# Denominators' absolute value and 128x1 products on another engine, with a new order of issue, in an xLSTM and mixture-of-experts kernel

## The chip, the cores and the metric

The kernel runs on one core of one Trainium2 chip. The metric is device time in microseconds (us) of one execution; a profiled execution is also known by its span, the time from the first to the last instruction of the program.

The engines are TensorE (PE in the profile, with PEld for its weight loads), VectorE (DVE), ScalarE (ACT), GpSimd (POOL) and SyncE (SP, which only issues transfers here).

## The reference

Three layers follow each other. The first is a recurrent attention over 768 positions of 2 batches and 8 heads of width 40, the second a feed-forward layer with a rational activation, the third a dense mixture of 4 experts with a ReLU.

```python
def _attn_ref(q, k, v, i_gate, f_gate, o_gate):
    for t in range(S):
        m_new = np.maximum(f_gate[:, :, t] + m, i_gate[:, :, t])
        f_stab = np.exp(f_gate[:, :, t] + m - m_new)
        i_stab = np.exp(i_gate[:, :, t] - m_new)
        C = f_stab * C + i_stab * outer(vt, kt)
        n = f_stab * n + i_stab * kt
        h_tilde = C @ qt
        denom = np.maximum(np.abs(n @ qt), 1.0)
        y[:, :, t] = sigmoid(o_gate[:, :, t]) * h_tilde / denom

def _moe_ref(x, w_in, w_out, a, b):          # x: 1536 x 320, w_in: 320 x 2048
    h = x @ w_in
    P = a[0] + a[1] * h + a[2] * h**2 + a[3] * h**3
    Q = 1.0 + np.abs(b[0]) * np.abs(h) + np.abs(b[1]) * h**2
    return (P / (Q + 1e-06)) @ w_out

def _moe2_ref(x, domain_probs, w1, w2):      # 4 experts, 320 x 1024 and 1024 x 320
    p = domain_probs / (domain_probs.sum(-1, keepdims=True) + 1e-09)
    for e in range(4):
        out += p[:, e:e + 1] * (np.maximum(x @ w1[e], 0.0) @ w2[e])
    return out
```

## The kernel before

The attention is done in chunks of 128 positions: 12 steps, 6 chunks of 2 batches. A step broadcasts the decays of the gates over the partitions (tiles `bc`, `bf`, `cb` in PSUM), turns them into a triangular weight with a scan (`fb`, line 710), multiplies the scores `sc` with it (L742), and sums the state's and the chunk's contributions in `o` (L756 and L762). Column 40 of each head of `o` is the product with the state's norm, and from it `s_pv` makes the 8 denominators of a row: `den` is max(-o, 1) by L764, then the larger of that and max(o, 1) by L765. `s_y` takes the reciprocal (L790), multiplies it into the output gate, and this into `o`. `s_x` transposes the result into `x`, as a high and a low half (L807 to L810), because every matrix product is made from two halves so that it keeps more bits.

Beside these steps the weights of the second layer are loaded and converted (`conv64`, tiles `cv_p`, `cv_l`, `cv_t`, `win`, `wout`). The second layer then runs in blocks of 256 tokens: first products `h` (L829), the rational activation `e_mono` (L853 to L868), second products `acc` (L841). It needs `x`, and `sb1`, the square root of |b[1]|, which `small_consts` makes on 128x1 tiles: an approximate square root and one step of Newton (L672 to L679). The first expert has the same form (L829, L877, L841); experts 1 to 3 use fewer products on sums of blocks (L1152), with second products at L1186. At the very end 6 accumulators `acc[t]`, each the sum of many products of L1186, are each scaled and added to `so` by VectorE (`evac_exp`, L953) and sent out by SyncE (L955).

What sets the order. Program text emits units in the order of the list `EMIT`. For each engine, `ORDER` then gives a permutation of the numbers of its own instructions, counted from 0 as they were emitted, and each instruction is tied behind the one in front of it in that list. An engine works its list strictly in order. `CHOICE` holds one letter for each use of a small operation that several engines could do (V VectorE, A ScalarE, G GpSimd), in the order of use: `ge` the masked copies of the gates, `gm` and `gl` other gate products, `ke` the products `kend` of keys and decay, `vi` the copies of the input gate, `low` and `hi` parts of the conversion, `ri` the linear part of the rational activation, `su`, `mh`, `ml` its sums and halves, `ws` the sums of weights for experts 1 to 3. `SPINS` says how many products of the identity with itself (L591, into a tile that is about to be written) are put ahead of which product.

```python
def spin(t, key):
    for _ in range(SPINS.get(key, 0)):
        PE.matmul(t[:, 0:P], spin_in, spin_in, start=True, stop=True)
...
# second(), the last 36 products of TensorE in order of emission, t = 0 to 5, six each
if k == NK - 1 and a == 1 and n == 2:
    evac_exp(e, b * NC + p * NH + w, acc[t])
```

Of the kernel before, what the change touches and what calls it, by code (L numbers as in the profile page):

```python
# [10 lines left out]
AF = mybir.ActivationFunctionType  # L11
ALU = mybir.AluOpType
# [23 lines left out]
    861-876 841-844 995 989 996 990-991 997 992 998 993 999 994 1000 880-895 1001 877-879 1002-1005 1007 1006 1008
    1013-1014 1009-1012 1019 920 896-911 949-960 1020 1015 1021 1016 1022 1017-1018 1023-1024 933-948 1025 1034 1028
    1026-1027 1040-1042 1029-1030 1035-1036 1031 1037-1038 1032-1033 1039 1049 1043-1047 1050-1053 1048 961-976 1055
    1082-1083 1054 1098-1100 1084 1079-1080 1101-1102 1081 1085-1086 1056-1059 1061-1065 1060 1066 1073-1074
    1130-1132 1067-1069 1075 1070 1076 1071 1077-1078 1072 1181-1196 1103-1113 1087-1097 1197-1212 1114-1129 1235  # L40
    1229-1232 1236-1237 1233 1238-1240 1234 1247 1241 1248-1249 1242 1250-1251 1243-1244 1213-1217 1252 1245-1246
    1218-1228 1133-1140 1733 1727 1734-1735 1728-1730 1736 1731 1737-1738 1732 1141-1142 1253-1267 1317 1268
    1143-1148 1323-1325 1318 1326 1319-1321 1327-1328 1322 1269-1284 2343 2349 2344-2345 2350-2351 2346 2352 2347
    2353-2354 2348 1329 1335 1330-1331 1336-1338 1332-1333 1339-1340 1334 1401 1285-1299 1149 1300 1402 1407 1403
    1408 1404-1405 1409-1411 1406 1412 1419 1413-1414 1420-1421 1415-1416 1422-1423 1417-1418 1424 1301-1316 2355
    2361-2363 2356 1463-1465 1457-1458 1466-1467 1459-1461 1468 1462 1341-1356 2364-2366 2357-2360 1165-1180 1150
    1425-1440 1357 1709 1703-1705 1710 1706 1389-1390 1711-1712 1707 1713-1714 1708 1151-1155 1358-1360 1156 1391
    1361 1392 1441-1456 1157-1160 1362-1365 1393-1394 1507-1508 1469-1471 1161-1164 1366-1368 1395-1400 1513
    1509-1510 1514-1515 1511 1516-1517 1512 1518 1472-1478 1519 1369 1525 1479-1487 1721 1715 1722 1716 1723-1724
    1717-1718 1488-1490 1725 1719 1726 1720 1526 1520-1521 1527-1529 1522-1523 1530 1524 1559-1571 1531 1572-1574  # L50
    1532 1537-1538 1373-1374 1539-1541 1533-1536 1542 1599-1614 1575 1581 1375-1377 1576-1579 1582-1583 1580
    1584-1586 1593-1597 1587-1591 1598 1592 1370-1372 1378-1388 1615-1630 1820 1814-1815 1821 1816 1822 1817 1823
    1818 1824 1819 1825 1669 1663-1664 1670 1665-1666 1671-1673 1667 1674 1668 1631-1634 1675 1681 1635-1645
    1676-1677 1682 1491-1498 1646 2041 1683 1678 1684-1686 2042 1679-1680 1499-1506 2047-2048 1687-1702 1543-1548
    2043 2049 2044-2046 2050-2052 1647-1650 1549-1552 1651-1652 1739-1741 1764 1758-1760 1765-1766 1653 1767
    1553-1557 1742-1757 1770 1776 1771-1772 1558 1654 1777-1778 1773 1779 1774 1780 1775 1781 1761 1768 1762-1763
    1769 1782-1797 1829 1835-1838 1830-1832 1839 1833 1840 1834 1655-1659 1798-1813 1841 1847-1848 1842 1849-1850
    1897 1660-1662 1843 1898-1903 1844 1851 1845 1852 1846 2146-2147 2140 2148 2141 2149 2142 2150 2143 2151 1853
    1826-1828 1904 2144 1905-1906 2145 1859-1860 1854-1855 1861 1907-1911 1862-1863 1856-1857 1864 1858 1865-1880
# [1256 lines left out]
```

## Time and profile before

| | |
|---|---|
| time, median of 3 runs | 631.87 us (630.75 to 633.73) |
| the profiled execution's own time | 631.61 us |
| its span | 629.8 us |
| mean granted clock of TensorE | 0.985 of full |
| TensorE busy | 609.9 us, 4417 instructions |
| VectorE busy | 479.0 us, 834 instructions |
| ScalarE busy | 367.4 us, 671 instructions |
| GpSimd busy | 274.1 us, 304 instructions |

Busy time is the time in which at least one instruction of the engine runs. Rows of a group of instructions give the busy time of the group and the mean duration of one; instructions of one engine can overlap, so that the first is less than the second times the count. Idle time stands behind, with what ended it.

### The profile page before, as it was taken

What the parts mean: (1) busy time and instruction counts of PE and PEld (TensorE: products, weight loads), DVE (VectorE), ACT (ScalarE), POOL (GpSimd) and SP (SyncE); (2) the same over time, 40 slices, a digit from 0 to 9 for tenths busy, and PEclk for the clock granted to TensorE, in tenths of its full rate; (3) what the DMA queues carried; (4) which work ended last, traced back from release to release, by engine and by line L of the source; (5) the groups of instructions that cost most, each with busy time, mean ns of one, the idle gap of its engine ahead of it and who ended that gap; (6) DMA issues with size and microseconds to landing.
All of it is one profiled execution on the core that took longest, in us unless ns stands there. A gap on an engine that the chain in (4) does not pass through costs nothing.

```text
span 629.8 us, 11629 instructions
## 1 busy us (share of the span) xinstructions
PE 609.9 (97%) x4417; PEld 596.2 (95%) x4417; DVE 479.0 (76%) x834; ACT 367.4 (58%) x671; POOL 274.1 (44%) x304
## 2 busy tenths in 40 slices
PE   7689999999999999999999999999999999999996
PEld 6678999999999999999999999989999999999996
DVE  7989999999989879787789855877555467643634
ACT  3888888747886866666678536425443253523231
POOL 5697888856643352132321237323552233531010
PEclk9679999999999999999999999999999999999999
DMA  7876344030312000000000120222120011100101
GB/s 207 275 231 170 113 120 119 21 119 2 88 42 71 1 1 2 2 1 1 1 2 22 39 81 21 55 65 69 39 69 15 14 37 46 41 2 0 63 1 62
DMA packets 21959, 36.65 MB, mean 58 GB/s; under 512 B 3568, under 2 KB 14320, under 8 KB 21904
## 3 DMA queue, kind: packets, MB, share of 16 engines
q1 hardware_dynamic: 21904, 35.92, 19.4%
q8 instruction: 34, 0.56, 0.4%
q14 instruction: 21, 0.17, 0.1%
HBM read 32.76 MB, written 1.97 MB: 55 GB/s over the span
## 4 chain that ended last, share of the span: by engine, by line
PE 86%; DVE 7%; issue 1%; DMA 1%; POOL 1%; SPq 1%; ACT 1%; DVEq 0%; ACTq 0%; POOLq 0%
PE h L829 21%; PE acc L841 20%; PE acc L1186 19%; PE h L1152 18%; PE o L762 2%; PE sc L737 2%; PE tx L807 1%; PE o L756 1%; DVE fb L710 1%; DMA stg_a<-in_moe_w_in_dram 1%; DVE gbc L331 1%; PE dl L777 1%; PE bf L649 1%; SPq L1078 1%; DVE cv_t L452 1%
## 5 line engine op out<-in xcount | busy, mean ns | idle before, releaser
L1152 PE MATMUL h<-ar,ar 128*128 128x384 f32 (+1 forms) x408 | 107.2, 341 | 0.7 <-DVE ar L1173 0.7
L829 PE MATMUL h<-x,win 128*128 128x256 f32 x768 | 104.5, 284 | 0.0
L841 PE MATMUL acc<-wout,g 128*128 128x320 f32 x576 | 101.2, 313 | 0.0
L1186 PE MATMUL acc<-ar 128*128 128x320 f32 x432 | 100.0, 309 | 0.8 <-ACT ar L1168 0.8
L829 PEld LDWEIGHTS h<-x,win 128*128 128x128 f32 x768 | 98.2, 191 | 1.0 <-DVE s__1241 L868 0.2
L1186 PE MATMUL acc<-ar,ar 128*128 128x320 f32 x432 | 98.2, 309 | 0.4 <-DVE ar L1173 0.4
L1168 ACT ACTIVATE ar<-h 128x384 fp32r<-128x384 f32 x72 | 35.3, 490 | 94.5 <-DVE h L1245 33.9
L841 PEld LDWEIGHTS acc<-wout,g 128*128 128x128 f32 x576 | 87.3, 189 | 1.1 <-POOL g L331 0.3
L1186 PEld LDWEIGHTS acc<-ar 128*128 128x128 f32 x432 | 74.7, 188 | 1.3 <-ACT ar L1168 1.3
L1186 PEld LDWEIGHTS acc<-ar,ar 128*128 128x128 f32 x432 | 74.0, 188 | 1.1 <-DVE ar L1173 0.7
L1152 PEld LDWEIGHTS h<-ar,ar 128*128 128x128 f32 (+1 forms) x408 | 71.6, 188 | 2.4 <-DVE ar L1173 1.1
L1173 DVE SCALAR_TENSOR_TENSOR ar<-h,ar 128x384 fp32r<-128x384 f32 x72 | 40.0, 556 | 35.3 <-ACT ar L1168 28.9
L1241 POOL TENSOR_TENSOR ar<-c,ar 128x384 fp32r<-128x384 f32 x24 | 24.4, 1015 | 79.5 <-ACT ar L1240 73.1
L1152 PE MATMUL h<-x,ar 128*128 128x384 f32 x216 | 57.5, 340 | 0.0
L829 PE MATMUL h<-x,we 128*128 128x256 f32 x384 | 56.3, 284 | 0.0
L829 PEld LDWEIGHTS h<-x,we 128*128 128x128 f32 x384 | 51.5, 191 | 0.1
L841 PE MATMUL acc<-we,g 128*128 128x320 f32 x288 | 49.7, 310 | 0.0
L841 PEld LDWEIGHTS acc<-we,g 128*128 128x128 f32 x288 | 43.6, 188 | 0.2 <-DVE g L878 0.2
L1152 PEld LDWEIGHTS h<-x,ar 128*128 128x128 f32 x216 | 37.3, 188 | 1.0 <-ACT s L1222 0.3
L1226 DVE TENSOR_TENSOR u<-h,s 128x384 f32<-128x384 f32 x24 | 13.3, 556 | 26.7 <-PE h L1152 22.1
L1238 ACT ACTIVATE c<-c 128x384 f32<-128x384 f32 x24 | 12.5, 522 | 36.0 <-DVE c L1237 36.0
L762 PEld LDWEIGHTS o<-v,fb 128*128 128x128 f32 x192 | 25.1, 201 | 3.9 <-DVE fb L742 3.3
(818 smaller groups left out, 1278.5 us busy)
## 6 DMA issues: line engine op xcount, KB each, us to landing
stg_b<-in_moe_w_out_dram SPq DMA_DIRECT2D x10, 512.0 KB
stg_a<-in_moe_w_in_dram SPq DMA_DIRECT2D x8, 512.0 KB
kv<-in_kv_dram SPq DMA_DIRECT2D x12, 320.0 KB
qkt<-in_qk_dram SPq DMA_DIRECT2D x24, 160.0 KB
stg_w<-in_moe_w_dram SPq DMA_DIRECT2D x12, 320.0 KB
stg_m<-in_moe_w_dram SPq DMA_DIRECT2D x24, 128.0 KB
stg_r<-in_moe_w_dram SPq DMA_DIRECT2D x72, 32.0 KB
so<-in_o_gate_dram SPq DMA_DIRECT2D x6, 320.0 KB
```

Source lines behind the costliest of these rows:

```text
L331: return ENG[alt(kind)].tensor_tensor(out=out, in0=in0, in1=in1, op=op)
L737: PE.matmul(sc[j][:, p, :], qkt[b][r, p, 2 * j], qT[r, p], start=True, stop=True)
L762: PE.matmul(o[:, h, :], st["W"][:, h, :], v1[:, h, :], start=(c == 0 and h == 0), stop=(h == H - 1))
L829: PE.matmul(o, w5[:, j, fs], r, start=(n == 0), stop=(n == len(seq) - 1))
L841: PE.matmul(acc[t], x, y, start=(first and a == 0 and n == 0), stop=(last and a == nff - 1 and n == 2))
L1152: PE.matmul(bank, w, x, start=(first and n == 0), stop=(n == 3), skip_group_check=True)
L1168: A.activation(g[:, 0], c, AF.Relu)
L1173: V.scalar_tensor_tensor(out=g[:, 1], in0=c, scalar=0.0, in1=g[:, 0].bitcast(F32), op0=ALU.max, op1=ALU.subtract)
L1186: PE.matmul(acc[t], g[:, x, w * P:(w + 1) * P], wo[:, y, a], start=(k == 0 and a == 0 and n == 0), stop=(k == NK - 1 and a == 1 and n == 2))
L1226: V.tensor_tensor(out=u2, in0=bb, in1=s1, op=ALU.add)
L1238: A.activation(c22, c22, AF.Relu)
L1241: G.tensor_tensor(out=g22[:, 1], in0=c22, in1=g22[:, 0].bitcast(F32), op=ALU.subtract)
```

## The change

In `small_consts` four operations on 128x1 tiles go from VectorE to ScalarE; the reciprocal and the maximum stay. In `s_pv` the absolute value of the 8 denominators is made by ScalarE from PSUM, and VectorE then takes the maximum with 1 in SBUF. Many letters of `CHOICE`, the counts of `SPINS`, and all five lists of `ORDER` are new; `EMIT` is the same. The numbers of `SPINS` add up to 203 before and 135 after.

```diff
@@ small_consts
         A.activation(rb1, ab1, AF.Abs_reciprocal_sqrt)
-        V.tensor_tensor(out=sb1, in0=ab1, in1=rb1, op=ALU.mult)
+        A.activation(sb1, ab1, AF.Copy, scale=rb1)
         V.reciprocal(rb1, sb1)
-        V.tensor_tensor(out=rb1, in0=rb1, in1=ab, op=ALU.mult)
-        V.tensor_tensor(out=sb1, in0=sb1, in1=rb1, op=ALU.add)
-        V.tensor_scalar(sb1, sb1, 0.5, None, op0=ALU.mult)
+        A.activation(rb1, rb1, AF.Copy, scale=ab)
+        A.activation(sb1, sb1, AF.Identity, bias=rb1)
+        A.activation(sb1, sb1, AF.Copy, scale=0.5)
@@ s_pv
             den = st["den"] = at2.tile([P, H, 1], F32, tag="den", name=f"den{i}")
-            V.tensor_scalar(den, o[:, :, D:D1], -1.0, 1.0, op0=ALU.mult, op1=ALU.max)
-            V.scalar_tensor_tensor(out=den, in0=o[:, :, D:D1], scalar=1.0, in1=den, op0=ALU.max, op1=ALU.max)
+            A.activation(den, o[:, :, D:D1], AF.Abs)
+            V.tensor_scalar(den, den, 1.0, None, op0=ALU.max)
@@ CHOICE, a part
-    gm="GG",
+    gm="VG",
-    gl="VGVVV",
-    ge="GAGAGAAAGAAG",
+    gl="VVVVV",
+    ge="AAAAAAAAGAAG",
-    low="AGAAAAAAAAAAGAAAAAAA",
-    hi="GGAAAAAAAAAAAAAAAAAAAAAG",
+    low="GAAAAAAAAAAAAAAAAAAA",
+    hi="GGGAAAAGAAAAAAAAAAAAAAGG",
-    vi="AGAAGAAAAAAA",
-    ke="GVVVGGGGGGVGGGGGGGGG",
+    vi="AAAAAAAGGAGA",
+    ke="GVVGGGGGGGVGGGGGGGGG",
@@ SPINS
-    bc0_1=21, bc1_1=43, sc0_0=9, sc0_1=60, sc1_0=4, sc1_1=19, bf2_0=1, dl0=1, o0=5, sc2_0=4,
-    sc2_1=1, o1=1, ist2=7, dl1=5, tx0=4, bf3_1=1, sc3_1=1, tx2=14, o5=1, dl5=1,
+    bc0_1=42, bc1_1=21, sc0_0=3, sc0_1=1, sc1_0=17, sc1_1=4, bf2_0=1, dl0=1, o0=14, sc2_0=1,
+    sc2_1=1, o1=1, ist2=2, dl1=2, tx0=9, bf3_1=2, sc3_1=1, tx2=9, o5=2, dl5=1,
@@ ORDER, the end of PE's list (the 6 accumulators' products are 4105 to 4140 before, 4037 to 4072 after)
-    4136-4137 4131-4133 4116 4138 4134 4128 4139-4140 4122
+    4036 4026 4016 4046 4051 4055 4067 4052 4056-4057 4061 4047 4053 4062 4068 4058 4063-4065 4059 4039 4048
+    4069-4070 4066 4071-4072 4060 4054 4040-4042
@@ ORDER, the end of DVE's list (the 6 additions of L953 are 828 to 833 before, 822 to 827 after)
-    826 825 827 833 832 828-829 831 830
+    796-797 790 786 795 798-818 820 819 821 823 827 826 822 824-825
```

## Rows read from the trace of the kernel before

**Rows 1.** Page: TensorE's busy time, and its granted clock in 40 slices (tenths).

```profile
PE 609.9 (97%) x4417; PEld 596.2 (95%) x4417; DVE 479.0 (76%) x834; ACT 367.4 (58%) x671; POOL 274.1 (44%) x304
...
PEclk9679999999999999999999999999999999999999
```

**Rows 2.** Windows: busy us (count) of each engine in stretches, granted clock, DMA.

```profile
core 0: us, PE busy (x) PEld busy (x) DVE busy (x) ACT busy (x) POOL busy (x), PEclk, DMA share, GB/s
0.00:20.90 20.90, 15.09 (x175) 13.39 (x175) 16.88 (x35) 10.05 (x23) 12.50 (x28) 1.00 0.75 222
...
32.90:35.90 3.00, 1.22 (x12) 1.11 (x11) 3.00 (x7) 2.52 (x6) 3.00 (x4) 1.00 0.82 241
38.00:44.70 6.70, 6.44 (x40) 5.67 (x40) 5.07 (x12) 5.41 (x13) 5.72 (x10) 0.50 0.82 249
44.70:64.00 19.30, 18.38 (x165) 16.94 (x165) 18.83 (x36) 15.86 (x32) 14.74 (x18) 1.00 0.56 149
64.00:300.00 236.00, 235.88 (x1858) 231.36 (x1858) 211.02 (x351) 176.35 (x315) 123.59 (x130) 1.00 0.16 47
...
415.00:425.00 10.00, 8.79 (x51) 7.98 (x50) 7.92 (x17) 1.77 (x4) 0.92 (x2) 1.00 0.34 95
...
620.00:629.80 9.80, 4.26 (x30) 3.99 (x28) 3.40 (x7) 0.14 (x1) 0.00 (x0) 0.93 0.29 100
```

**Rows 3.** Windows: the stretch from the first scores to the first rational activation.

```profile
20.00:54.00 34.00, 28.42 (x216) 25.93 (x215) 31.81 (x60) 29.07 (x59) 25.77 (x33) 0.75 0.77 234
```

**Rows 4.** Groups of VectorE by line, 0 to 57 us.

```profile
L331 DVE TENSOR_TENSOR gbc<-gbc 16x384 fp32r<-16x384 f32 (+1 forms) x4 | 2.3, 586 | 0.1
...
L331 DVE TENSOR_TENSOR kend<-kv,fb 128x160 f32<-128x160 f32 x3 | 1.2, 412 | 0.0
...
L678 DVE TENSOR_TENSOR sb<-sb,rb 128x1 f32<-128x1 f32 x1 | 1.1, 1065 | 0.0
...
L677 DVE TENSOR_TENSOR rb<-rb,ab 128x1 f32<-128x1 f32 x1 | 0.5, 484 | 0.0
L764 DVE TENSOR_SCALAR den<-o 128x8 f32<-128x8 f32 x3 | 0.5, 158 | 0.0
...
L331 DVE TENSOR_TENSOR ga<-ga 16x128 fp32r<-16x128 f32 x1 | 0.3, 285 | 0.0
...
L675 DVE TENSOR_TENSOR sb<-ab,rb 128x1 f32<-128x1 f32 x1 | 0.3, 255 | 0.0
...
L679 DVE TENSOR_SCALAR sb<-sb 128x1 f32<-128x1 f32 x1 | 0.2, 153 | 0.0
```

**Rows 5.** Timeline around L678: start us, us, what (VectorE, then GpSimd).

```profile
50.99 1.06 DVE L678 TENSOR_TENSOR sb<-sb,rb 128x1 f32<-128x1 f32 x1
...
50.75 1.29 POOL L331 TENSOR_TENSOR wout<-cv_t,wout 128x512 fp32r<-128x512 f32 x1
```

**Rows 6.** Groups of ScalarE by line, 0 to 60 us.

```profile
L325 ACT ACTIVATE win<-cv_t 64x512 fp32r<-64x512 f32 (+1 forms) x8 | 5.0, 624 | 2.7 <-DVE cv_t L452 1.9 <-DVE gbc L621 0.8
L449 ACT ACTIVATE cv_l<-stg_a 128x512 int16<-128x512 uint8 x6 | 4.7, 782 | 0.0
...
L325 ACT ACTIVATE fm<-gbc,mask 112x384 fp32r<-112x384 f32 x3 | 1.7, 601 | 0.7 <-DVE gbc L331 0.7
...
L325 ACT ACTIVATE cm<-ga,mask 48x128 fp32r<-48x128 f32 x2 | 0.8, 394 | 0.6 <-DVE ga L331 0.6
...
L325 ACT ACTIVATE v<-ist 128x8 f32<-128x8 f32 x3 | 0.6, 215 | 0.0
...
L674 ACT ACTIVATE rb<-ab 128x1 f32<-128x1 f32 x1 | 0.2, 203 | 0.0
```

**Rows 7.** Timeline of the end: start us, us, what, count, idle before.

```profile
621.90 1.33 PE L1186 MATMUL acc<-ar 128*128 128x320 f32 x8
...
623.95 0.31 PE L1186 MATMUL acc<-ar,ar 128*128 128x320 f32 x1
624.15 2.84 DVE L953 SCALAR_TENSOR_TENSOR so<-acc,pr,so 128x320 f32<-128x320 f32 x6 [3.04 <-PE acc L1186]
```

More of the change, by code (lines that the diff above doesn't have):

```diff
@@ new lines @@
+    1113-1128 1033-1045 1003-1004 1018-1024 1129-1136 1025-1027 1046-1049 1137 1161 1138-1140 1167 1141-1144
+    1050-1061 1168-1170 1162 1173 1163 1171 1028 1145 1164 1172 1165-1166 1146-1154 1659 1665 1660 1666-1667 1661
+    1155-1160 1065-1066 1662 1668 1179-1180 1174-1175 1181-1184 1176-1178 1185-1190 1669-1670 1663-1664 1067-1071
+    1191-1200 1072-1080 1255-1257 1249-1250 1258 1251-1253 1259-1260 1254 2281 2275 2282 2276 1201-1205 2277-2278
+    1206-1216 2283-2285 2279 2286 2280 1261 1267 1262 1268 1263-1264 1269-1271 1265 1272 1266 1029 1217-1232
@@ new lines @@
+    1333-1334 1339-1340 1335-1337 1341-1343 1338 1344 1351 1345-1346 1352-1353 1347-1348 1354-1355 1349-1350 1356
+    1233-1248 1081-1082 2287-2289 1083-1086 1097 1395 1389 1396-1397 1390 1398 1391-1393 1399-1400 1394 1273-1288
+    2290 2293-2297 2291 2298 2292 1098-1112 1357-1372 1635 1641 1636 1642 1637-1640 1643-1646 1321 1289-1296
+    1322-1323 1373-1388 1297 1087-1095 1324-1326 1401-1403 1439-1440 1096 1441 1298-1303 1327-1332 1445 1442
+    1446-1449 1443-1444 1450 1404-1405 1457 1451-1452 1406-1419 1647-1649 1458-1460 1453-1455 1461-1462 1456
@@ new lines @@
+    1977-1978 1579-1591 1671-1673 1592 1480-1482 1983-1984 1483-1490 1674-1689 1702-1703 1708-1709 1704 1710-1711
+    1690 1696 1691-1692 1697 1693 1698-1700 1694 1701 1695 1705 1712 1706-1707 1713-1729 1593 1761 1767-1770
+    1762-1764 1771 1765-1766 1772 1730-1744 1779 1773 1780 1774 1781-1782 1745 2072 2078 1594 1775-1777 1783
+    2079-2080 2073 2081 2074 2082 2075-2077 2083 1784 1778 1829-1841 2116 2122 1758 2123 2117 1759-1760 1791 1785
+    1792-1793 1786-1787 1794-1795 1788-1789 1796 1790 1797-1812 1845 2124 2118 2125 1842-1844 1867 1861-1862
@@ new lines @@
+    1859-1860 2010 2005 2011-2012 2006 2044-2059 1953-1957 2025-2029 2231 2013 2237 2232 2238 2030-2032 2014-2016
+    2019 2084-2099 1958-1960 2033-2040 2239-2240 2233 2241 2234-2236 2242 2020-2021 2017 2022-2023 2018 2024
+    2100-2115 2185 2179 2186-2187 2180-2181 2188-2189 2182 2190 2183-2184 2128-2130 2299 2305 2300-2301 2306 2302
+    2307-2308 2303 2309 2304 2310 2471 2465 2472 2163-2178 2473-2475 2466-2468 2476 2469-2470 2207 2213 2208
+    2214-2216 2209 2217 2210-2212 2218 2131-2132 2259-2274 2219 2225 2220-2222 2226-2228 2223 2229 2224 2230
@@ L207 @@
[L207 removed]
+    12-13 19 18 41 20 26 16 25 17 15 31 14 30 42 46 23 32 38 21 40 22 33 24 34 39 27-28 49 29 47-48 36 35 53 37 50
+    43 52 45 56 51 57 44 54 58 55 59 62 60-61 65-66 63 67 64 71 68 72 75 69-70 76-77 74 73 79 78 82 81 80 90-95 103
+    108 106 100 110 109 97 96 105 99 101 98 104 107 102 111-113 118 115 114 116-117 120 119 121 126-127 125 128 133
+    122 129 134-135 124 130-131 123 132 136 139 138 137 141 140 142-144 148 145 153 152 146-147 151 149 156 150 154
@@ L208 @@
+    159 158 155 157 160-162 169 163 168 166 165 170-171 167 164 177 173-176 172 180 178 181-182 184 179 188-189
+    186-187 185 183 194 190-192 195 193 197 196 198 205 204 202-203 200-201 199 207 206 212 208 214 210 213 211 209
+    215 217 219 218 216 220 222 226 225 221 223-224
     """,
```

343 lines of the change are left out of this document (158 added, 185 removed).

## The prediction

> **What bounds the kernel now.** I read the page first. TensorE is busy for 609.9 us of a span of 629.8 [rows 1], so what any other engine saves can count only where TensorE waits, or where it runs at the lower of its two clocks (the page shows less than full clock only near the start and in the last slice). The windows tell where that is [rows 2]. From 64 to 300 us TensorE is busy for 235.88 of 236 us: nothing is to be had there. [...] In the first 20.9 us it idles for 5.8 us, behind the gates' chain. [...] From 415 to 425 us it idles for 1.21 us, where experts 1 to 3 begin. In the last 9.8 us it is busy for 4.26.
>
> The third view is the stretch from 20 to 54 us, where the attention has to deliver the first `x` and the second layer has to get going [rows 3]. VectorE is busy for 31.81 of 34 us there and ScalarE for 29.07, so VectorE has 2.2 us left and ScalarE 4.9. The fourth is the groups of VectorE and ScalarE by line, for prices [rows 4, 6], and the fifth the timeline of the end [rows 7].
>
> **The change, part by part: the front.** I counted each engine's instructions as the program emits them, with the new letters, and read the lists of ORDER with these numbers. What stands ahead of the first L860, VectorE's first operation of the rational activation (97th in VectorE's list before, 91st after)? Eight entries go. They are three of L764 at 0.158, one product `kend` at 0.41 (letter `ke`, to GpSimd), and the four 128x1 operations, at 0.26, 0.48, 1.06 and 0.15 [rows 4]. That is 0.47 + 0.41 + 1.95 = 2.83 us. Two entries come, from GpSimd: a gate product of 48x128, for which VectorE's 16x128 at 0.285 is the nearest row, and a difference of 16x384 at 0.586, 0.87 us together. L765 stays as the maximum, at about its old price. The net is -1.96 us. For the second `x`, which stands further ahead, only two L764, the `kend` product and L675 have gone, 0.32 + 0.41 + 0.26, against the same 0.87: -0.12 us. So the first products `h` hardly start earlier, and the rest must come from the rational activation behind them.
>
> What does ScalarE get ahead of its first L853 (79th before, 88th after)? Twelve come: two masked copies of 48x128 at 0.394, one of 112x384 at 0.60, one copy of 128x8 at 0.215, one `cv_l` at 0.78, three absolute values of 128x8, priced like that copy at 0.215 (the floor is the 0.203 of a 128x1), and the four operations on 128x1 at 0.203 [rows 6]. That is 3.84 us. Three go, a `cv_l` and two conversions at 0.62, or 2.03 us. Net +1.81 us, which fits into its 4.9 us of idle time [rows 3]; if that cover were gone, all 1.81 us would stand in the path (a rival below).
>
> So the front's gain lies between nothing and 1.96 us. From 44.7 to 64 us TensorE has only 0.92 us of idle time that an earlier activation could fill [rows 2], and I take that bound: -0.9 us.
>
> The odd price is L678: 1.06 us for 128 numbers, next to a GpSimd product from 50.75 to 52.04 that ends when it does [rows 5]. [...]
>
> **The order of the first 20 us.** The decays of batch 1 (`bc1`) and the gates' three transposes now stand in TensorE's list ahead of the 8 score products of step 0, which therefore wait for VectorE's zeroing of gate columns; behind them the `o` products of step 0 wait too. VectorE's own list has the gates' reciprocal ahead of the first scan L710, as before, with two gate operations shifted in front of it. I take 0 for this, and a microsecond either way. The 68 fewer fillers stand in front of products that wait for VectorE and ScalarE, so I cost them at nothing; were TensorE not waiting, they would be a gain.
>
> **The order of the end.** This can be read off the lists. Before, the last entries of PE are 4116, 4138, 4134, 4128, 4139, 4140, 4122. Six products belong to each accumulator, so these hold the last one of t = 1, 4, 3, 5 and 2, in places 7, 5, 4, 2 and 1 from the end. VectorE's additions come in the order t = 5, 4, 0, 1, 3, 2, so all six wait for the product in place 2. The trace shows it: the six start at 624.15, against a TensorE end of 624.26, and take 2.84 us, until 626.99 or 2.73 us behind TensorE [rows 7]. After, the last products of t = 1, 4, 5, 3, 2, 0 stand in places 11, 8, 6, 5, 4, 1, and VectorE goes t = 1, 5, 4, 0, 2, 3. A product of this kind takes 0.146 us, (1.33 - 0.31) / 7 [rows 7], and an addition 0.47, 2.84 / 6. t = 1 can begin 1.4 us ahead of TensorE's end and t = 5 0.7 us ahead; t = 4 then ends at +0.25, and t = 0, 2, 3 follow until +0.25 + 3 x 0.47 = +1.7 us. That is 2.73 - 1.7 = 1.0 us less. The outputs leave in the same order, each behind its addition, so the end of the span moves with them: -1.0 us.
>
> **The middle.** The letters `ws` and SyncE's order at the start of experts 1 to 3 are new. The 1.21 us of idle time there can go or double; 0, with 1.2 either way.
>
> **Sum.** 629.8 - 0.9 - 1.0 = 627.9 us of span. The profiled execution took 631.61, 1.8 us more than its span, so 629.7; the median of the runs is 0.26 above it. That makes 630.0 us.
>
> **The rivals.**
>
> *The front is hidden.* VectorE gains only 0.12 us ahead of the second `x`, and if the first activation waits for ScalarE's or GpSimd's part, nothing else is left: 631.87 - 1.0 = 630.9 us. For it speaks the 18.38 of 19.3 us that TensorE is busy from 44.7 to 64 us [rows 2].
>
> *The slow clock goes away.* The stretch at 0.50 follows 3 us, 32.9 to 35.9, in which TensorE was busy for 1.22 only [rows 2]. Both broadcasts of step 2 now stand together ahead of the `o` products of step 1, and the fillers ahead of the first transposes grow from 4 to 9. If these fill the hole, half of 6.44 us goes as well: 630.0 - 3.2 = 626.8 us. Against it: in that hole TensorE waits for VectorE, whose list is only 0.12 us shorter by then.
>
> *ScalarE becomes the bound of the front: slower.* An engine's list is strict. Each absolute value now waits in ScalarE's list for the last product of `o`, and the sigmoids, conversions and the high half of `x` queue behind it; TensorE waits for that half. If ScalarE's 1.81 us come on the path, TensorE gets a hole in 44.7 to 64 us like the 1.8 us one of 32.9 to 35.9, and this decides: a hole of that size was followed by the half clock, for 3.2 us. 631.87 - 1.0 + 1.8 + 3.2 = 635.9 us. Against it speak ScalarE's 4.9 us of idle time [rows 3]. [...]
>
> **Chances.** About 0.5%, 3.2 us, is what a measurement of this kernel can tell from no change: faster is below 628.7, slower above 635.0. The forecast gets 0.40, the hidden front 0.17 (both are within 0.5%), the clock 0.30, ScalarE 0.13. So faster 0.30, the same 0.57, slower 0.13. The forecast's own range is 628.8 to 632.0, by a microsecond for the first 20 us and the middle's 1.2. The whole range reaches to the clock's case and its microsecond below, 626.0, and upward to 633.5; it leaves out the slower case and the outer part of the fast one.
>
> **What would show it.** The six L953 should no longer start together: VectorE should end 1.7 us behind TensorE's last product. L675, L677, L678, L679 should be on ScalarE at 0.2 to 0.3 us, L764 at about 0.2. From 44.7 to 64 us TensorE's idle time should shrink, with ScalarE's busy share from 20 to 54 us up by 1.8 us. The prediction is wrong if the stretch at 0.50 before 45 us vanishes or a new one appears behind 45 us, if TensorE waits in 44.7 to 64 us for ScalarE by more than 2 us, or if the idle time from 415 to 425 us moves by more than 1.2 us.

## The result, and the profile after

The changed kernel takes 638.13 us (637.45 to 639.66, 12 runs) where the kernel before takes 633.25 (630.71 to 636.97, 12 runs beside it): a ratio of 1.0085, with a 95% interval of 1.0065 to 1.0104. It is slower by 0.85%, some 5 us. Ratios that follow are to the kernel before, measured on the same chip in the same session. The profiled execution of the changed kernel took 637.47 us with a span of 635.7, the one of before 631.61 with 629.8.

The page of the changed kernel; these lines answer to [rows 1]:

```profile
PE 609.8 (96%) x4349; PEld 594.9 (94%) x4349; DVE 488.0 (77%) x828; ACT 361.7 (57%) x675; POOL 278.9 (44%) x307
...
PEclk8569999999999999999999999999999999999999
```

TensorE is as busy as before, with 68 instructions fewer. VectorE has 6 instructions fewer and is busy for 9.0 us more. Most of that is other work, by the new letters: of the linear part of the rational activation (`ri`) VectorE now does 11 operations of 0.80 us instead of 4, 5.6 us more. The 12 maxima take 3.0 us more, and their first step, 1.9 us, has gone to ScalarE. The clock is lower in the first slices (8, 5 and 6 tenths in the first, second and third where 9, 6 and 7 stood). Line numbers behind `ORDER` are one higher than before (L829 is now L830).

The windows of the changed kernel, to set against [rows 2] (same columns):

```profile
0.00:20.90 20.90, 11.45 (x108) 9.80 (x108) 17.20 (x37) 11.64 (x28) 12.00 (x26) 0.80 0.80 224
20.00:36.00 16.00, 10.89 (x72) 10.32 (x73) 15.69 (x25) 13.18 (x25) 9.56 (x12) 0.59 0.76 230
34.50:37.40 2.90, 0.06 (x1) 0.00 (x0) 2.90 (x6) 2.40 (x5) 1.09 (x2) 0.85 0.83 252
36.70:46.60 9.90, 9.20 (x52) 8.18 (x52) 6.74 (x13) 6.63 (x15) 7.55 (x11) 0.50 0.80 246
44.70:64.00 19.30, 17.89 (x159) 16.46 (x157) 16.91 (x30) 16.04 (x38) 14.70 (x21) 0.95 0.52 142
64.00:300.00 236.00, 233.30 (x1825) 227.22 (x1826) 213.86 (x343) 167.18 (x305) 130.66 (x140) 1.00 0.16 49
64.00:380.00 316.00, 312.43 (x2418) 306.08 (x2419) 280.73 (x440) 218.46 (x393) 154.78 (x160) 1.00 0.15 43
415.00:425.00 10.00, 10.00 (x63) 9.72 (x63) 7.11 (x14) 4.23 (x8) 5.23 (x5) 1.00 0.23 64
380.00:440.00 60.00, 58.67 (x365) 56.88 (x364) 42.25 (x82) 27.87 (x50) 30.79 (x28) 1.00 0.17 45
```

and three of the same windows of the kernel before, which were not shown:

```profile
20.00:36.00 16.00, 10.68 (x82) 9.62 (x81) 15.72 (x30) 13.85 (x27) 11.14 (x15) 0.68 0.87 271
64.00:380.00 316.00, 315.88 (x2451) 311.11 (x2451) 274.20 (x447) 226.38 (x400) 145.30 (x155) 1.00 0.15 42
380.00:440.00 60.00, 58.07 (x352) 55.61 (x351) 45.38 (x81) 29.64 (x53) 26.87 (x21) 1.00 0.20 54
```

The 5.9 us of span can be put together from these. From 64 to 380 us TensorE now idles for 3.57 us where it idled for 0.12: +3.45. From 380 to 440 it idles for 1.33 instead of 1.93: -0.60. The end, below, gives -1.0. That leaves +4.1 us for the first 64 us. There, weighing TensorE's busy time by the granted clock (an estimate: busy time times one minus the clock, in windows of 1 us), 5.0 us more are lost to the half clock (11.6 instead of 6.6) and 4.2 us more to idling (16.5 instead of 12.3), and the fillers, weighed by the clock in the same way, take 5.2 us less (10.4 instead of 15.6): some 4 us in all, which agrees. Half clock means a granted clock of 0.50: in windows of 0.25 us both traces show 0.50 or 1.00, and another value only in the 5 windows of each in which the clock changes. In the kernel before the 16 score products of 38 to 44.5 us, at 0.50, keep TensorE busy for 2.1 us, and the 32 of 45 to 64 us, at 1.00, for 2.3.

Who TensorE waits for in the first 80 us of the changed kernel (waits of the engine, longest first):

```profile
PE bc L601 <- ACT cm L326: 3.5, 1, 3.5
PE o L592 <- DVE x L796: 2.8, 1, 2.8
PE o L763 <- DVE fb L743: 2.8, 1, 2.8
...
PE o L763 <- ACT win L326: 2.0, 1, 2.0
```

And VectorE and GpSimd around the hole of 34.5 to 37.4 us (timeline):

```profile
31.93 0.19 DVE L791 RECIPROCAL den<-den 128x8 f32<-128x8 f32 x1
...
33.84 1.45 POOL L332 TENSOR_TENSOR wout<-cv_t,wout 128x512 fp32r<-128x512 f32 x1
...
34.19 1.45 DVE L332 TENSOR_TENSOR so<-so,den 128x320 f32<-128x320 f32 x1
...
36.87 0.47 DVE L796 TENSOR_TENSOR x<-o,so 128x320 f32<-128x320 f32 x1
...
37.40 0.26 PE L592 MATMUL o<-ident 128*128 128x128 bf16 x1 [2.84 <-DVE x L796]
```

The same steps of the kernel before (timeline):

```profile
31.47 0.19 DVE L790 RECIPROCAL den<-den 128x8 f32<-128x8 f32 x1
...
32.22 0.20 DVE L684 TENSOR_TENSOR pr<-pr,psum__548 128x48 f32<-128x48 f32 x1
...
32.53 0.90 POOL L328 TENSOR_SCALAR fm<-gbc,mask 112x384 fp32r<-112x384 f32 x1
32.57 0.49 DVE L331 TENSOR_TENSOR so<-so,den 128x320 f32<-128x320 f32 x1
...
34.12 0.48 DVE L795 TENSOR_TENSOR x<-o,so 128x320 f32<-128x320 f32 x1
```

From the end of the denominators' reciprocal to the start of the first `x` VectorE needs 2.46 us before and 4.75 after. Seven instructions stand between the two in both lists, but not the same ones: after, a weighted score `fb` (0.68), a second conversion `cv_t` (0.68) and a gate difference (0.85) stand where two `kend` products and a small reciprocal stood. So part of the delay is the order itself; 0.96 us of it is `so`, which takes 1.45 us beside a GpSimd product (33.84 to 35.29), and took 0.49 beside a GpSimd copy (L328, 32.53 to 33.43).

The maximum of the denominators, all 12 of it (duration in ns, minimum / median / maximum): first before, reading PSUM, then after, reading SBUF. As groups of VectorE they are busy for 1.9 us before and 4.9 after (busy us, mean ns). The third line is the first step of before, an instruction of the same form (TENSOR_SCALAR) and size as the one after, but reading PSUM.

```profile
L765 DVE SCALAR_TENSOR_TENSOR den<-o,den x12: 150/158/167, 30.7 to 161.9; 128x8 f32<-128x8 f32 x12
```

```profile
L765 DVE SCALAR_TENSOR_TENSOR den<-o,den 128x8 f32<-128x8 f32 x12 | 1.9, 159 | 0.1
```

```profile
L764 DVE TENSOR_SCALAR den<-o x12: 148/156/167, 27.8 to 161.7; 128x8 f32<-128x8 f32 x12
```

```profile
L766 DVE TENSOR_SCALAR den<-den x12: 143/168/1171, 31.3 to 166.3; 128x8 f32<-128x8 f32 x12
```

```profile
L766 DVE TENSOR_SCALAR den<-den 128x8 f32<-128x8 f32 x12 | 4.9, 408 | 1.6 <-ACT den L765 1.6
```

Seven of the 12 after began well within a GpSimd instruction, and each of these ends 0.03 us behind it, after 0.14 to 1.17 us; the other five take 0.16 to 0.17. The longest of them beside GpSimd's product (timeline of the changed kernel): it ends when that does, and TensorE idles behind the `x` that follows it.

```profile
88.40 1.29 POOL L332 TENSOR_TENSOR win<-cv_t,win 128x512 fp32r<-128x512 f32 x1
...
88.54 1.17 DVE L766 TENSOR_SCALAR den<-den 128x8 f32<-128x8 f32 x1
...
89.63 0.55 DVE L811 TENSOR_TENSOR x<-tx,x 128x384 fp32r<-128x384 f32 x1
...
90.23 0.50 PE L650 MATMUL cb<-cm,selc 112*128 112x512 f32 x1 [0.81 <-DVE x L811]
```

The end, against [rows 7]: the last product of TensorE ends at 631.18, the last addition of VectorE at 632.87, 1.69 us later instead of 2.73.

```profile
629.75 0.55 DVE L954 SCALAR_TENSOR_TENSOR so<-acc,pr,so 128x320 f32<-128x320 f32 x1 [2.27 <-PE acc L1187]
...
630.43 0.75 PE L1187 MATMUL acc<-ar,ar 128*128 128x320 f32 x4
630.49 2.38 DVE L954 SCALAR_TENSOR_TENSOR so<-acc,pr,so 128x320 f32<-128x320 f32 x5 [0.18 <-PE acc L1187]
```

### The profile page after: what moved, and what is told of

It is laid out like the page before. It is cut to its first block, busy times and chain, and to the rows that moved or that the text cites. A ratio compares the mean times of both kernels' runs of the same rounds, so it can differ in the third digit from the quotient of the medians.

```text
span 635.7 us, 11472 instructions
## 1 busy us (share of the span) xinstructions
PE 609.8 (96%) x4349; PEld 594.9 (94%) x4349; DVE 488.0 (77%) x828; ACT 361.7 (57%) x675; POOL 278.9 (44%) x307
## 4 chain that ended last, share of the span: by engine, by line
PE 72%; DVE 18%; ACT 3%; issue 3%; POOL 2%; DMA 1%; SPq 1%; DVEq 0%; ACTq 0%; POOLq 0%
PE acc L1187 20%; PE h L1153 18%; PE h L830 15%; PE acc L842 14%; DVE fb L711 2%; DVE h L868 1%; DVE fb L743 1%; DMA stg_b<-in_moe_w_out_dram 1%; PE o L763 1%; DVE cv_t L453 1%; PE tx L808 1%; DVE we L332 1%; PE sc L738 1%; DVE x L811 1%; DVE qc L719 1%
## 5 line engine op out<-in xcount | busy, mean ns | idle before, releaser
L830 PE MATMUL h<-x,win 128*128 128x256 f32 x768 | 105.9, 285 | 0.8 <-DVE x L811 0.6
L1187 PE MATMUL acc<-ar 128*128 128x320 f32 x432 | 101.4, 310 | 0.5 <-ACT ar L1169 0.5
L830 PEld LDWEIGHTS h<-x,win 128*128 128x128 f32 x768 | 98.4, 191 | 2.2 <-DVE x L811 0.8
L830 PE MATMUL h<-x,we 128*128 128x256 f32 x384 | 57.5, 284 | 0.5 <-DVE we L332 0.5
L830 PEld LDWEIGHTS h<-x,we 128*128 128x128 f32 x384 | 51.9, 191 | 0.8 <-DVE we L332 0.8
L842 PE MATMUL acc<-we,g 128*128 128x320 f32 x288 | 51.0, 311 | 0.9 <-DVE g L879 0.9
L1153 PEld LDWEIGHTS h<-x,ar 128*128 128x128 f32 x216 | 37.4, 188 | 0.5
L332 POOL TENSOR_TENSOR stg_r<-stg_r 96x128 f32<-96x128 f32 x29 | 13.3, 464 | 41.8 <-DMA stg_r<-in_moe_w_dram 27.9
L763 PEld LDWEIGHTS o<-v,fb 128*128 128x128 f32 x192 | 26.5, 215 | 5.4 <-DVE fb L743 3.0
L763 PE MATMUL o<-v,fb 128*128 128x41 f32 x192 | 26.8, 299 | 4.8 <-DVE fb L743 2.8
```

The costliest lines, as they stand in the source:

```text
L332: return ENG[alt(kind)].tensor_tensor(out=out, in0=in0, in1=in1, op=op)
L763: PE.matmul(o[:, h, :], st["W"][:, h, :], v1[:, h, :], start=(c == 0 and h == 0), stop=(h == H - 1))
L830: PE.matmul(o, w5[:, j, fs], r, start=(n == 0), stop=(n == len(seq) - 1))
L842: PE.matmul(acc[t], x, y, start=(first and a == 0 and n == 0), stop=(last and a == nff - 1 and n == 2))
L1153: PE.matmul(bank, w, x, start=(first and n == 0), stop=(n == 3), skip_group_check=True)
L1187: PE.matmul(acc[t], g[:, x, w * P:(w + 1) * P], wo[:, y, a], start=(k == 0 and a == 0 and n == 0), stop=(k == NK - 1 and a == 1 and n == 2))
```

## The experiments

Two theories stood at the start. "Operations": the moved operations themselves cost. "Lists": the new letters, fillers and orders cost. Where lists of both kernels are joined, each keeps its own letters on its side of the cut.

### The operations alone, and undone

The operations in the lists of before:

```diff
@@ s_pv, lists of before
-            V.tensor_scalar(den, o[:, :, D:D1], -1.0, 1.0, op0=ALU.mult, op1=ALU.max)
-            V.scalar_tensor_tensor(out=den, in0=o[:, :, D:D1], scalar=1.0, in1=den, op0=ALU.max, op1=ALU.max)
+            A.activation(den, o[:, :, D:D1], AF.Abs)
+            V.tensor_scalar(den, den, 1.0, None, op0=ALU.max)
...
@@ small_consts: the four operations to ScalarE, as in the change
```

> The kernel before, all its letters, fillers and lists kept; only the four 128x1 operations and the absolute value of the denominators go to ScalarE, each put into ScalarE's list where it started in time before. Theory 'lists': the 4.9 us that the change lost come from its new lists and letters, so this one is within 1 us of the kernel before. Theory 'operations': the maximum with 1, which now reads SBUF, is stretched (in the changed kernel the 12 of them take 4.9 us where the 12 that read PSUM took 1.9), and ScalarE's list waits for the products of o; then this one is slower than before by 2 to 4 us.

Measured: 1.0031 (1.0007 to 1.0054), span 631.9: the theory of the operations holds here, at its lower end. The maximum in this run:

```profile
L775 DVE TENSOR_SCALAR den<-den x12: 160/180/1084, 30.5 to 163.9; 128x8 f32<-128x8 f32 x12
```

The same edit the other way round, in the lists of the change:

> The changed kernel with its letters, fillers and lists; the four 128x1 operations and the denominators' first step back on VectorE, at the places in its list where ScalarE had started them. Theory 'lists': still slower than the kernel before by 4 to 5.5 us. Theory 'operations': at least 3 of the 4.9 us come back, so slower than before by less than 2 us.

Measured: 1.0092 (1.0068 to 1.0116). So the lists cost by themselves, and the two costs do not add. In its profile, what the maximum had cost behind the front comes back (from 64 to 380 us TensorE idles for 2.51 instead of 3.57 us), but the front is later: TensorE's score products that start at 50.04 us in the changed kernel start 1.77 us after that. That the undone operations on VectorE do this is not shown: VectorE is 0.72 us behind at 27 us already, and the first of them runs at 31.91.

### The maximum from PSUM

```diff
-            V.tensor_scalar(den, den, 1.0, None, op0=ALU.max)
+            V.scalar_tensor_tensor(out=den, in0=o[:, :, D:D1], scalar=1.0, in1=den, op0=ALU.max, op1=ALU.max)
```

In the lists of before:

> As the kernel with only the operations moved, in the lists of before, but the maximum reads the denominators of o from PSUM again, in the form of before: the larger of max(o, 1) and the absolute value that ScalarE made. The result is the same. Theory 'port': the maximum of the earlier run was stretched because it read only SBUF beside GpSimd's products (4.6 us for 12, longest 1.08); here all 12 take 0.15 to 0.2 us, and the span comes back from 631.9 to 630.3 or less, the time to within 0.7 us of before. Rival 'handover': ScalarE's step in the chain of the denominators is what costs; then the time stays about 1.6 to 2 us above before.

Measured: 0.9995 (0.9974 to 1.0016), span 629.7. "Port" holds in its times, 0.146 to 0.168 us for all 12 (by what mechanism, no run shows); "handover" falls: ScalarE still makes the absolute value, and the four small operations are still on ScalarE. The maximum reads `o` in PSUM again, and it is the instruction of before with two inputs again; that the price goes with the memory and not with the form is shown by L764 above, which has the form of the slow one and takes at most 0.167 us from PSUM. At 96.65 and at 145.52 us of the kernel before it starts within a GpSimd product, takes 0.16 us, and ends 0.64 and 0.65 us ahead of that product.

```profile
L775 DVE SCALAR_TENSOR_TENSOR den<-o,den x12: 146/158/168, 30.3 to 162.0; 128x8 f32<-128x8 f32 x12
```

In the lists of the change:

> The changed kernel, but the maximum of the denominators reads o in PSUM again and takes the larger of max(o, 1) and ScalarE's absolute value; all else kept. In the lists of before this gave back the whole 2 us that the moved operations had cost. If the costs add, it gives back 1.5 to 2 us here too, to 3 to 4 us above before. If the new lists have their bound elsewhere (fillers, copies on GpSimd, the start), less than 0.7 us: the kernel with the operations undone was no faster than the changed one.

Measured: 1.0043 (1.0026 to 1.0061), 635.51 us. About 0.42%, 2.6 us, of the loss comes back (0.26% either way, from the two intervals); the rest is the lists'. Beside the 1.0092 of the operations undone, this also says that in the new lists the moved operations are worth some 0.5% (0.3% either way), once the maximum reads PSUM.

### Where in the lists

Everything that had started by a given time in one kernel first, the rest in the order of the other:

> Everything that had started in the first 64 us of the kernel before stands first, with its engines, fillers and lists (with VectorE's denominators of steps 0 to 3 and the 128x1 operations on VectorE); all the rest follows with the letters and in the order of the changed kernel. Theory 'front': TensorE has lost 4.3 us against before by 68 us in the changed kernel, and only 1.5 us net behind it; so this one is slower than before by 1 to 2.5 us. Rival 'steady state': it is the new letters and lists behind 64 us that cost, and this one is slower by 4 us or more.

> The reverse: everything that had started in the first 68 us of the changed kernel stands first, with its letters, fillers, operations and lists; the rest follows as in the kernel before. Theory 'front': slower than before by 3.5 to 5 us. Rival 'steady state': slower by less than 2 us.

Measured: front of before with the rest of the change 1.0054 (1.0027 to 1.0081), 3.4 us, between what the two theories gave, with an interval that reaches into both; front of the change with the rest of before 1.0067 (1.0042 to 1.0092), 4.2 us, as theory 'front' had it. Both halves seemed to cost. With the maximum from PSUM in the first of them this cleared up:

> The kernel with the first 64 us of before and the changed kernel behind, and the maximum of steps 4 to 11 from PSUM. Theory 'front': what is left of the loss lies in the first 65 us; then this one is within 1 us of before (of the idle time behind 64 us, 0.8 us at 87 us goes with the maximum, 2.3 us at 184 and 350 stay, 1.7 us come back behind 400). Rival 'rest': it stays 2.5 us or more above before.

Measured: 1.0003 (0.9975 to 1.0030). Behind 64 us the lists of the change cost nothing net that can be told, once the maximum is mended: in this profile TensorE still idles for 2.5 us from 64 to 380 us, and 0.6 us in the middle and 1.0 at the end are gained. What is left of the loss is in the front. Two cuts in it, with the operations of before except for step 0's denominators in the second:

> Everything that had started in the first 20.4 us of the changed kernel stands first, with its letters, fillers and lists; all the rest as in the kernel before (operations too). Theory 'start': the order of the first 20 us, with 116 fillers fewer ahead of the scores and transposes, makes the clock fall at 12.8 instead of 20.9 us in every run, and this costs 2 to 3 us. Theory 'VectorE's lists behind': within 1 us of before, as the prediction had it, with a mean clock of 0.984 or more in most runs.

> The same with the first 36 us of the changed kernel (to the hole at 34.5 to 37.4 us), and the rest as in the kernel before. Theory 'start': no more than 0.7 us above the kernel with the first 20 us alone. Theory 'VectorE's lists': 1.5 us or more above it, and 2 to 4 us above before. With all of the first 68 us of the changed kernel it was 1.0067 of before, 4.2 us.

Measured: the first 20.4 us alone 1.0021 (1.0007 to 1.0036), the first 36 us 1.0088 (1.0064 to 1.0112). So the first 20 us cost 1.3 us, between the two theories, with a mean clock of 0.971 to 0.980 in all 12 runs. (By the counts of `SPINS` 62 fillers are gone in it, not the 116 of the expectation.) With the first 36 us it is 4.2 us more, the way "VectorE's lists" had it, but 5.6 us in all, more than that theory gave, and no less than the first 68 us of the change cost (4.2). VectorE and GpSimd in the second of them (timeline):

```profile
34.32 1.45 POOL L341 TENSOR_TENSOR wout<-cv_t,wout 128x512 fp32r<-128x512 f32 x1
...
34.67 1.45 DVE L341 TENSOR_TENSOR so<-so,den 128x320 f32<-128x320 f32 x1
...
35.75 1.38 POOL L338 TENSOR_SCALAR cm<-gbc,mask 112x384 fp32r<-112x384 f32 x2
...
36.04 2.39 DVE L694 TENSOR_TENSOR pr<-pr,psum__481 128x48 f32<-128x48 f32 x1
...
37.10 1.26 POOL L341 TENSOR_TENSOR wout<-cv_t,wout 128x512 fp32r<-128x512 f32 x1
...
39.01 0.47 DVE L809 TENSOR_TENSOR x<-o,so 128x320 f32<-128x320 f32 x1
```

Two products of VectorE with both inputs in SBUF take 3.84 us, where they took 0.49 and 0.20 in the kernel before; `x`, which reads `o` in PSUM, takes its usual 0.47 but comes late, and TensorE waited 3.3 us for it. In the changed kernel `pr` takes 0.20 us (at 35.55), so the stall of 2.39 is not one of the changed kernel's: it comes with the joined lists. This run shows what such a stall costs, but it is no price for 20 to 36 us of the changed kernel. That price is an estimate by difference: 0.43% is left with the maximum from PSUM, 0.21% is the first 20 us, nothing net lies behind 64 us, so some 0.2%, 1.4 us, is left for 20 to 64 us, with at least 0.2% of uncertainty either way.

### Single suspects in the front

`x0` earlier, in VectorE's list (41 is the reciprocal, 42 the product `so`, 43 `x0`; six operations stand between them, not the five of the expectation):

```diff
-    ... 41 83 75 46 42 57 89 48 43 38 ...
+    ... 41 42 43 83 75 46 57 89 48 38 ...
```

> The changed kernel with two entries of VectorE's list moved: the product of step 0's output gate with the reciprocal, and x0 itself, go right behind the reciprocal, ahead of the five operations that stand between them (two parts of weight conversions, a gate operation, a normalisation, a weighted score). Theory 'lists': the hole of 2.8 us in TensorE at 34.5 to 37.4 us (o waits for x0) goes, the stretch of half clock behind it gets shorter, and the time falls by 2 to 4 us against the changed kernel, to 1 to 3 us above the kernel before. Rival: the wait moves on to the copy of x0 by ScalarE or to the next conversion, and the time falls by less than 0.7 us.

Measured: 1.0104 (1.0081 to 1.0128), span 636.4: no gain; the rival's size holds, by another wait than it named. `x0` was there at 33.1 us, and now TensorE waited 3.8 us for the weighted score `fb` that stands behind. The stall had moved to the next product with two SBUF inputs, `pr`, 1.16 us instead of 0.20 (timeline):

```profile
34.88 1.44 POOL L342 TENSOR_TENSOR wout<-cv_t,wout 128x512 fp32r<-128x512 f32 x1
...
35.23 1.16 DVE L695 TENSOR_TENSOR pr<-pr,psum__479 128x48 f32<-128x48 f32 x1
...
37.64 0.27 PE L602 MATMUL bf<-ident 128*128 128x128 bf16 x1 [3.78 <-DVE fb L753]
```

More fillers, in the start and beside the hole:

```diff
-    ... o0=14 ... ist2=2 ...
+    ... o0=72 ... ist2=22 ...
```

> The changed kernel with more fillers where TensorE idles in the first 16 us: 72 instead of 14 (key o0) ahead of the broadcasts that wait 3.5 us for ScalarE's masked copies, and 22 instead of 2 (key ist2) ahead of the gates' transposes. In the changed kernel the granted clock falls to half at 12.8 us, in the profile of before at 20.9, and all 12 runs of the changed kernel have a mean clock of 0.972 to 0.978 where most of before's have 0.984 to 0.986. Theory 'fillers': the 68 removed fillers are what lets the clock fall early; with them back the mean clock rises to 0.98 or more and the time falls by 2 to 3.5 us against the changed kernel, to 2 to 3.5 us above before. Rival: TensorE only waits in those 20 us, the early half clock is hidden (the first products of the scores start 1.0 us later than before, and those of step 1 only 0.6), and the time falls by less than 0.7 us.

```diff
-    ... dl1=2 ...
+    ... dl1=40 ...
```

> The changed kernel with 40 instead of 2 fillers (key dl1) ahead of the state products of step 1, beside the hole of 2.8 us at 34.5 to 37.4 us that ends when VectorE has made x0; the hole becomes some 0.6 us, and the state products come 2.3 us later. Theory 'clock of the hole': the second stretch at half clock (36.7 to 46.6 us) goes or shrinks by half, and the time falls by 2 to 4.5 us. Rival: the clock falls as before, the state products or what waits for them are late, and the time stays within 0.7 us or rises by up to 1.5.

Measured: 1.0101 (1.0073 to 1.0128) and 1.0074 (1.0047 to 1.0101); neither is faster than the changed kernel beyond the uncertainty, so the rivals hold in the time; that the clock would fall as before, as the second had it, does not. The first adds 78 fillers at two places, mostly not those from which the change took its own (59 at key sc0_1). The fillers did raise the clock where they stand, without a gain in time. Windows of the changed kernel, of the one with more fillers at the start, and of the one with more beside the hole:

```profile
12.80:20.90 8.10, 4.28 (x25) 2.89 (x24) 7.31 (x15) 5.35 (x13) 6.63 (x11) 0.50 0.76 251
...
36.00:52.00 16.00, 14.60 (x104) 13.17 (x103) 12.39 (x22) 12.31 (x28) 11.35 (x17) 0.68 0.64 197
```

```profile
12.80:20.90 8.10, 5.66 (x46) 4.78 (x46) 7.40 (x13) 4.89 (x14) 5.52 (x9) 0.79 0.67 231
...
36.00:52.00 16.00, 13.18 (x76) 11.87 (x76) 11.83 (x20) 12.20 (x28) 10.46 (x14) 0.57 0.61 194
```

```profile
36.70:46.60 9.90, 8.69 (x55) 7.42 (x55) 7.51 (x14) 7.05 (x16) 7.69 (x11) 0.66 0.84 274
...
58.00:72.00 14.00, 11.65 (x77) 10.37 (x77) 9.34 (x17) 9.11 (x20) 10.32 (x14) 0.76 0.35 93
```

With fillers at the start the clock of 12.8 to 20.9 us rises from 0.50 to 0.79, and that of 36 to 52 falls from 0.68 to 0.57. With fillers beside the hole 36.7 to 46.6 rises to 0.66, and 58 to 72 us, at full clock in the changed kernel, is at 0.76.

Two letters of the front taken back, both with the maximum from PSUM:

```diff
-    xd="AAG...
+    xd="AAA...
```

> The changed kernel with the maximum from PSUM, and one letter taken back: the copy of x2's last columns is ScalarE's again, ahead of a conversion in its list. On GpSimd it starts at 60.77 us, 1.4 us behind x2, and TensorE waits 0.75 us for it and then 0.85 for the x that follows. Theory 'front letters': the time falls by 0.8 to 1.5 us against the kernel with the maximum alone (which was at 1.0043 of before). Rival: another wait of this stretch takes its place, and it stays within 0.5 us.

```diff
-    gl="VVVVV",
+    gl="VGVVV",
```

> The changed kernel with the maximum from PSUM, and the gate difference of 16x384 (second letter of gl) back on GpSimd, where it stands behind a product kend and ahead of a conversion. VectorE, busy for 31.6 of 32 us from 20 to 36 us save 0.4, then has 0.55 us less ahead of the first weighted scores of step 1. Theory 'VectorE is the bound of the front': these come 0.5 to 1 us earlier, the hole at 34.5 to 37.4 us and the half clock behind it shrink, and the time falls by 0.5 to 1.5 us. Rival: GpSimd's copy takes longer (0.99 us before) and delays the masked copies, and the time stays or rises.

Measured: 1.0044 (1.0023 to 1.0065), the rival; and 1.0026 (1.0002 to 1.0050) against 1.0043, the expected direction, but within the uncertainty. In the second one's profile `x0` came at 37.02 us, no earlier than in the changed kernel: the product `so` still took 1.45 us.

### The end, the second half, and a better version

```diff
@@ ORDER, end of DVE's list, lists of before
-    826 825 827 833 832 828-829 831 830
+    826 825 827 829 833 832 828 830-831
...
@@ ORDER, ends of PE's and SP's lists likewise
```

> The kernel before, with the last 32 entries of TensorE's list, the last 7 of VectorE's and the last 7 of SyncE's in the changed kernel's order and nothing else. Theory of the prediction: VectorE ends 1.7 us behind TensorE's last product instead of 2.7, and the time falls by 1.0 us. Rival: the end is set by the transfers behind the last addition, and the time stays within 0.3 us of before.

Measured: 0.9977 (0.9961 to 0.9994), 1.5 us with 0.4 to 2.5 as its interval. VectorE ends at 626.70, 1.68 us behind TensorE's last product (timeline):

```profile
624.27 0.75 PE L1196 MATMUL acc<-ar,ar 128*128 128x320 f32 x4
624.32 2.38 DVE L963 SCALAR_TENSOR_TENSOR so<-acc,pr,so 128x320 f32<-128x320 f32 x5 [0.18 <-PE acc L1196]
```

> The kernel before for everything that had started there by 380 us, and the lists and letters of the changed kernel for what follows (the last products of the first expert, experts 1 to 3, and the end). TensorE's idle time from 380 us to the end is 7.5 us before and 5.8 us in the changed kernel; so the theory that the change's gain lies in this part gives 1.7 us less than before, 1.0 us of it the end and 0.6 the beginning of experts 1 to 3. Rival: the latter depends on where the conversions stand when the part begins; then only 1.0 us.

Measured: 0.9994 (0.9972 to 1.0015). Its interval, 1.8 us less to 0.9 us more, does not tell 1.0 from 1.7 us, nor either from nothing; its own profile has the idle time of both parts as in the changed kernel, in a span of 628.1.

> The kernel before with the end in the changed kernel's order, and 57 more fillers where TensorE waits in the first 20 us (66 instead of 43 of key bc1, 33 instead of 21 of bc0, 29 instead of 7 of ist2). About a third of the runs of before have a mean clock of 0.973 to 0.98 and take 3 us more than the others. Theory 'fillers': those runs become rare, so the median falls by 1.0 us for the end and up to 1 us more, and the spread narrows. Rival: the fillers only stand in the way, and it is no faster than the kernel with the end alone (0.9977 of before).

Measured: 0.9980 (0.9960 to 1.0001), no faster than the end alone: the rival, in the time. Half of the theory came true all the same: all 12 runs have a mean clock of 0.981 to 0.989, where the kernel before beside them has 0.974 to 0.988. So the clock's mean rose, and no gain in time followed that can be told.

> The version the runs point to: the kernel before with its lists, the four 128x1 operations and the absolute value on ScalarE, the maximum from PSUM, and the end in the changed kernel's order. The parts alone were at 0.9995 and 0.9977 of before. If they add: 0.997 to 0.998, 1.0 to 1.9 us less than before. If the end's gain depends on where VectorE stands: 0.999 to 1.0.

Measured: 0.9961 (0.9935 to 0.9987), 630.75 us beside 632.76. It beats both kernels; that it beats the end alone is not shown.

## Why the prediction was wrong

**The end: right.** -1.0 us was forecast from VectorE ending 1.7 us behind TensorE; it ends 1.69 behind, and alone this gave 0.9977.

**The middle: right within its bound.** 0 with 1.2 either way; 0.6 us of idle time came back between 380 and 440 us: TensorE waits for 0.67, 0.43 and 0.77 us at 386, 415 and 425 us before, and for 0.84 and 0.49 at 393 and 431 after. So one wait shrank, one went, and one grew.

**"L765 stays as the maximum, at about its old price": the first step that failed.** Its source went from PSUM to SBUF. From SBUF, seven of 12 lasted to the end of a GpSimd instruction beside them: 4.9 us for 12 instead of 1.9, longest 1.17. In the lists of before this cost 0.3%; in the lists of the change, mended, 0.4% came back, about half of the loss. The prediction had such a case in its row of L678, which took 1.06 us and ended with the GpSimd product beside it, and did not ask the same of the maximum. In the runs an instruction of the same form and size, 128x8, takes up to 1.17 us from SBUF, and at most 0.17 from PSUM. By what mechanism, no run shows.

**"-0.9 for the front": the second step that failed, wrong in sign.** The places that were counted were counted rightly, and the four operations cost 0.27, 0.29, 0.29 and 0.21 us on ScalarE, 1.06 instead of the 0.81 (4 x 0.203) assumed. With the maximum from PSUM and in the lists of before they gain nothing measurable (0.9995), so even there the front was "hidden". But the first rational activation came 2.06 us later (L854 at 56.20, L853 at 54.14 before). Two things were missing in the sum. It counted what stands ahead of the second `x` and of the first activation, not ahead of the first `x` (L795), for which TensorE then waits 2.8 us: VectorE's list has 59 instructions ahead of it before and 60 after, longer ones in part, and it starts 2.75 us later. And it kept old prices for instructions that now run beside GpSimd's products: `so` takes 1.45 us instead of 0.49 in the changed kernel, and `pr` 1.16 and 2.39 instead of 0.20 in two runs with entries moved. Ahead of the first L860 the durations of VectorE's instructions add up to 55.5 us before and 55.4 after, where -1.96 was forecast. VectorE is busy for 15.72 of 16 us from 20 to 36 us before and 15.69 after, so what it loses there it cannot make up. Which entry is to blame is not settled: the stall moves when an entry is moved. Nor are all waits of this kind. At 60.06 us VectorE idles for 1.62 us until ScalarE's part of a conversion is done, and ScalarE had idled for 1.53 us until the weights for it landed; no run varies the order of the front's transfers alone, so what this costs stays open.

**"0 for the first 20 us, a microsecond either way": somewhat too small.** 1.3 us, with 0.4 to 2.3 as its interval. That the missing fillers cost nothing was not tested at their own places; 78 others in the first 16 us gained nothing.

**"From 64 to 300 us nothing is to be had": a gain was excluded, a loss was not bounded.** 3.45 us of idle time arose from 64 to 380 us. 0.8 us at 90 us goes with the maximum from PSUM; 2.0 us (0.55 each at 181 and 184 us, 0.87 at 354) stay, in profiles with either front.

**The signs named.** The six L953 no longer start together, and the operations on ScalarE have the prices foreseen. But from 44.7 to 64 us TensorE's idle time grew from 0.92 to 1.41 us, ScalarE's busy time from 20 to 54 us fell from 29.07 to 27.46, and the stretch at half clock now lasts to 46.6 us.

**The rivals.** The slower one came nearest (635.9), by a mechanism that was wrong: ScalarE is not the bound. Its absolute value takes 0.166 us, VectorE fetched the first one 3.3 us after it was done, and in the lists of before the handover costs nothing that can be told. What fits it is that the hole in the front was followed by a longer half clock: 9.9 us at 0.50 behind a hole of 2.8, against 6.7 at 0.50 behind one of 1.8; two stretches are no rule. "The slow clock goes away" fell: all 12 runs of the change have a mean clock of 0.972 to 0.978. The 3.2 us for the half clock in the sums of these two rivals, half of 6.44, are an estimate that no run shows as time lost: with 0.66 instead of 0.50 from 36.7 to 46.6 us the time was at 1.0074, beside 1.0085.

## What to carry to other kernels

When an operand moves from PSUM to SBUF, price the instruction again: ask which GpSimd instructions will run beside it, and do not take its old row (0.16 us here): from SBUF it lasted to the end of the GpSimd instruction beside it, up to 1.17 us. On an engine without idle time count what stands ahead of the first result that another engine waits for, not only of later ones, and look at which of its instructions will run beside GpSimd's products. A stretch in which nothing is to be gained can still lose, and needs a bound on that side.

## What the runs showed of the hardware that was not expected

A VectorE instruction of 128x48 elements lasted over more than one GpSimd instruction in a row: `pr` took 2.39 us in the run with the first 36 us, from 36.04 to 38.43, over most of two masked copies and the whole of a product that ended at 38.36. So the longest of the GpSimd instructions beside it, 1.26 us, was no bound for what it took. And the clock: in the changed kernel, fillers that kept TensorE busy in one place raised the granted clock there (0.50 to 0.79 from 12.8 to 20.9 us; in the other run 0.50 to 0.66 from 36.7 to 46.6), and it was lower in a later one (0.57 instead of 0.68 from 36 to 52 us; 0.76 instead of 1.00 from 58 to 72). With those at the start, what the half clock took in the first 52 us, busy time times one minus the clock in windows that begin at 0, 12.8, 20.9 and 36 us, is estimated at 10.2 us where the changed kernel lost 11.3 by the same windows. In the kernel before, 57 more fillers raised the clock's mean (0.981 to 0.989 in 12 runs, beside 0.974 to 0.988), and no gain in time could be told (0.9980 with the new end, 0.9977 for the new end alone).
